# Two weight scalings moved, the first row tile's normalization split, and the last output tiles cut and shared out anew

## The chip, the cores and the metric

One core of a Trainium2 chip. The metric is device time in microseconds (us). TensorE is PE in the profile, its weight load PEld, VectorE is DVE, ScalarE ACT, GpSimd POOL, the SyncE queue SP; a "q" behind an engine is its sequencer, which issues transfers and waits.

## The reference

```python
xn = layernorm(x)                                      # x: [2048, 640] bf16
q  = (xn @ wq) as 32 heads of 192
s  = softmax(q k^T * 192**-0.5) v over the last 512 keys, all heads, then @ wo      # [2048, 640]
g  = silu( (sigmoid(xn @ w_gate) * (xn @ w_up)) @ w_down )
return x + s * g
```

## The kernel before

It starts with the gate branch (first four row tiles normalized and turned one by one, then the weights), goes through the query projection and attention in 16 rounds, and ends with the products with `wo` for the last eight row tiles. `row tile` is 128 rows of 640 columns. What the change touches:

```python
# start: row tile 0..3
def ln_apply(t):
    xn = xpool.tile([P, D], BF16, name="xn")
    nc.vector.tensor_scalar(xn[:], x_tiles[t], mv[:, t, 0:1], rstd[:, t, :],
                            op0=ALU.subtract, op1=ALU.mult)
    return xn
...
for q in range(TQ):
    if q + 1 < TQ: ln_part(q + 1, 0)                 # statistics of the next tile, first half
    nc.vector.reciprocal(rstd[:, q:q+1, :], ...)
    xn_t[q] = ln_apply(q)
    if q + 1 < TQ:
        ln_stats(q + 1, 1)                           # second half
        ln_sqrt(q + 1)                               # ScalarE
    if q == 0:
        turn(0); warm_up(NWARM[1]); continue         # TensorE transposes, ScalarE copies them out
...
# weights of the second pair of rounds: VectorE scales a chunk, GpSimd builds the sums, and loads
def scale_raw(g, c, on_act=True): ...                # 128x1536, bf16 -> fp16, in place
def second_w(c):
    copy_w(1, c, nc.gpsimd.tensor_copy)
    sum_w(1, c, nc.gpsimd.tensor_tensor, nc.gpsimd.tensor_copy)
    load_raw(1 + (c + 3) // NCD, (c + 3) % NCD, nc.gpsimd)
...
for n, k in enumerate((0, 1, 7, 2, 3, 8, 4, 5, 9, 6, 10)):   # query products of the first round
    slots[k]()
    if n == 2: ...
    elif n == 6:
        scale_raw(1, 2, on_act=False)
    if n in (0, 1, 6):
        second_w(min(n, 2))
...
    for k, x in enumerate(s_list):                   # score steps, with the next round's query products
        stage_s(r, *x, k)
        ...
        if r == 0 and k in (3, 7):
            scale_raw(1, 3 + k // 4, on_act=False)
            second_w(3 + k // 4)
...
# end
def finish(ps, gB_sb, t, d0, d1, on_pool=False, queue=nc.sync):
    o_sb = late["fout"].tile([P, D], BF16, name="o_sb")        # four buffers
    d = slice(d0, d1)
    if on_pool:
        tmp = late["tmp"].tile([P, D], F32, name="tmp")
        nc.vector.tensor_tensor(tmp[:, d], ps, gB_sb[:, d], ALU.mult)
        nc.gpsimd.tensor_tensor(o_sb[:, d], tmp[:, d], acc[t][:, d], ALU.add)
    else:
        nc.vector.tensor_tensor(ps, ps, gB_sb[:, d], ALU.mult)
        nc.vector.tensor_tensor(o_sb[:, d], ps, acc[t][:, d], ALU.add)
    queue.dma_start(of[t * P:(t + 1) * P, d], o_sb[:, d])

def stage_wo(r, i, q):
    ...
    if r == last and i * TQ + q == 2 * TQ - 1:       # the eighth of the last tiles, in three pieces
        cuts = [0, D // 2, D - P, D]
        for e, (d0, d1) in enumerate(zip(cuts, cuts[1:])):
            ps = ps_all[:, (4, 5, 0)[e], 0:d1 - d0]
            wo_mm(ps, r, i, q, [(d0, d1 - d0)], d0)
            finish(ps, gates[t], t, d0, d1, queue=nc.scalar)
        return
    ...                                              # GpSimd adds tiles 2, 4, 6 and 7 of the last eight
```

The softmax here doesn't subtract the row's maximum and nothing guards it: scores larger than these inputs give would overflow.

## Time and profile before

| before | |
|---|---|
| time, median of the first 3 runs | 905.09 us (904.78 to 905.09) |
| span of the profiled run | 902.9 us |
| TensorE busy | 896.0 us (99%) |
| first matmul at / last one ends at | 1.34 / 898.40 us |
| last transfer lands / program ends | 901.59 / 902.85 us |

An engine at 99% sets the time, so only its gaps count. If the middle hangs on TensorE alone, a gap that is closed early should arrive at the end in full.

### The profile page before, as it was taken

What the parts mean: (1) busy time and instruction counts of PE and PEld (TensorE: products, weight loads), DVE (VectorE), ACT (ScalarE), POOL (GpSimd) and SP (SyncE); (2) the same over time, 40 slices, a digit from 0 to 9 for tenths busy, and PEclk for the clock granted to TensorE, in tenths of its full rate; (3) what the DMA queues carried; (4) which work ended last, traced back from release to release, by engine and by line L of the source; (5) the groups of instructions that cost most, each with busy time, mean ns of one, the idle gap of its engine ahead of it and who ended that gap; (6) DMA issues with size and microseconds to landing.
All of it is one profiled execution on the core that took longest, in us unless ns stands there. A gap on an engine that the chain in (4) does not pass through costs nothing. (4 is left out here: it accounts for less than half of the span.)

```text
span 902.9 us, 18554 instructions
## 1 busy us (share of the span) xinstructions
PE 896.0 (99%) x7791; PEld 531.6 (59%) x7791; DVE 653.0 (72%) x1090; ACT 432.9 (48%) x511; POOL 178.8 (20%) x220
## 2 busy tenths in 40 slices
PE   9999999999999999999999999999999999999998
PEld 5545454556656565656565656566666666565665
DVE  5879956677677867786778677866786678666566
ACT  4323346764247633753376437643854285424240
POOL 0051112780001100110011001100110000001982
PEclk9999999999999999999999999999999999999999
DMA  9993384424554645373626362727293815263744
GB/s 284 269 268 92 97 146 104 119 55 87 87 91 59 144 76 102 60 143 69 109 56 147 57 119 46 157 54 123 31 172 45 132 23 129 39 120 130 159 128 121
DMA packets 188069, 100.38 MB, mean 111 GB/s; under 512 B 156176, under 2 KB 180368, under 8 KB 187984
## 3 DMA queue, kind: packets, MB, share of 16 engines
q1 hardware_dynamic: 158656, 57.69, 32.5%
q0 software_dynamic: 9408, 29.93, 14.2%
q10 hardware_dynamic: 19920, 11.57, 5.5%
q8 instruction: 61, 1.00, 0.5%
q14 instruction: 24, 0.20, 0.1%
HBM read 57.87 MB, written 5.24 MB: 70 GB/s over the span
## 5 line engine op out<-in xcount | busy, mean ns | idle before, releaser
L657 ACT ACTIVATE E<-ps_all 128x1024 bf16<-128x1024 f32 x256 | 252.7, 1022 | 303.0 <-PE ps_all L653 184.8
L714 PE MATMUL ps_all<-wo_g,oT 128*128 128x512 bf16 (+2 forms) x1542 | 228.3, 299 | 0.0
L653 PE MATMUL ps_all<-qT,kT 64*128 64x512 bf16 x1536 | 194.4, 376 | 0.0
L671 PE MATMUL ps_all<-v_sb,E 128*128 128x193 bf16 x2048 | 189.8, 247 | 0.1
L671 PEld LDWEIGHTS <-E 128*128 128x128 bf16 x2048 | 168.6, 98 | 18.7 <-issue 6.8
L714 PEld LDWEIGHTS <-oT 128*128 128x128 bf16 x1542 | 121.5, 98 | 78.4 <-issue 2.3
L584 DVE COPY qp<-ps_all 128x512 f32<-128x512 f32 x150 | 100.7, 688 | 58.4 <-PE ps_all L563 58.3
L601 DVE TENSOR_TENSOR qT<-ps_all,qp 128x512 bf16<-128x512 f32 x165 | 109.7, 688 | 45.7 <-PE ps_all L563 37.4
L653 PEld LDWEIGHTS <-kT 64*128 64x128 bf16 x1536 | 75.4, 94 | 89.2 <-issue 5.2
L678 DVE TENSOR_TENSOR o_st<-ps_all,rden 128x768 bf16<-128x768 f32 x120 | 114.9, 957 | 5.0 <-DMA oT<-o_st 0.9
L202 POOL DMA_DIRECT2D raw<-in_A_wq_dram x80 | 48.1, 606 | 276.2 <-ACT wB L224 238.9
L135 POOL DMA_DIRECT2D k_sb<-in_A_k_cache_dram x32 | 32.7, 1026 | 275.2 <-DVE o_st L678 155.6
L219 ACT ACTIVATE raw<-raw,w_sc 128x1536 f16<-128x1536 bf16 x37 | 58.3, 1575 | 1.9 <-DMA raw<-in_A_wq_dram 1.0
L497 PE MATMUL ps_all<-wd_sb,hT_sb 128*128 128x512 bf16 (+1 forms) x384 | 52.8, 299 | 0.0
L563 PE MATMUL ps_all<-XA,wA 64*128 64x512 f16 x420 | 51.9, 376 | 0.2 <-DVE qp L584 0.2
L563 PE MATMUL ps_all<-XB,wB 64*128 64x512 f16 x420 | 52.0, 376 | 0.0
L563 PE MATMUL ps_all<-X,w 64*128 64x512 bf16 x420 | 51.9, 376 | 0.0
L749 DVE TENSOR_TENSOR acc_lo<-ps_all,acc_lo 128x640 f32<-128x640 f32 x48 | 39.5, 823 | 15.9 <-PE ps_all L714 15.7
L453 DVE TENSOR_TENSOR hT_sb<-ps_all,sig_sb 128x512 bf16<-128x512 f32 x48 | 32.4, 683 | 22.0 <-ACT sig_sb L452 11.3
L677 DVE RECIPROCAL rden<-ps_all 128x4 f32<-128x4 f32 x128 | 23.2, 181 | 34.1 <-PE ps_all L671 32.7
L452 ACT ACTIVATE sig_sb<-ps_all 128x512 bf16<-128x512 f32 x48 | 28.0, 596 | 40.1 <-PE ps_all L447 37.1
L749 DVE TENSOR_TENSOR acc_hi<-ps_all,acc_hi 128x640 f32<-128x640 f32 x48 | 39.3, 819 | 7.7 <-PE ps_all L714 7.7
(118 smaller groups left out, 764.0 us busy)
## 6 DMA issues: line engine op xcount, KB each, us to landing
raw<-in_A_wq_dram POOLq DMA_DIRECT2D x80, 192.0 KB, 4.1
k_sb<-in_A_k_cache_dram POOLq DMA_DIRECT2D x32, 192.0 KB, 5.6
wo_g<-in_A_wo_dram ACTq DMA_DIRECT2D x6, 960.0 KB, 7.1
v_sb<-in_A_v_cache_dram ACTq DMA_DIRECT2D x28, 192.0 KB, 3.8
gB_d<-gB_sb POOLq DMA_DIRECT2D x16, 160.0 KB, 3.5
gBa_sb<-gB_d SPq DMA_DIRECT2D x16, 160.0 KB, 3.9
xa_sb<-in_A_x_dram SPq DMA_DIRECT2D x16, 160.0 KB, 3.9
out_dram<-o_sb SPq DMA_DIRECT2D x15, 160.0 KB, 1.9
```

The source lines that it names most:

```text
L202: eng.dma_start(raw[r], wq_r[:, c, :, g * GC:(g + 1) * GC])
L219: nc.scalar.activation(raw.bitcast(F16), raw, AF.Copy, scale=w_up)
L497: nc.tensor.matmul(oB_ps[:, d0:d0 + dsz], lhsT=hT_sb[:, f, q * P:(q + 1) * P], rhs=wd_sb[:, f, d0:d0 + dsz], start=(f == 0), stop=(f == NF ...
L563: nc.tensor.matmul(ps_all[:, b, :], lhsT=w(r, c), rhs=x[r, c, :], start=(first and k == 0), stop=(k == len(cs) - 1), skip_group_check=True,)
L584: nc.vector.tensor_copy(dst, part(b))
L601: nc.vector.tensor_tensor(q_out(i, u, pp), part(b), t, ALU.add)
L653: nc.tensor.matmul(ps[:, b, :], lhsT=kT[h, c * PC + j, :], rhs=qT_t[r][i, j][h, pp, :], start=(j == 0), stop=(j == PC - 1),)
L657: nc.scalar.activation(E_t[r, i, pp][:, c, :, :], ps, AF.Exp, scale=scale_qk)
L671: nc.tensor.matmul(o_ps[:, q // 2, q % 2, 0:DH + 1], lhsT=E[:, c, h, q * P:(q + 1) * P], rhs=vt[:, c, 0:DH + 1], start=(c == 0), stop=(c = ...
L678: nc.vector.tensor_tensor(o_st[:, :, h * DH:(h + 1) * DH].rearrange("p (b i) d -> p b i d", b=2), o_ps[:, :, :, 0:DH], rden[:].to_broadcas ...
L714: nc.tensor.matmul(oA[:, d0 - base:d0 - base + dsz], lhsT=oT_t[r, i, pp][:, q * PC + j, :], rhs=wo_t[runs[r][1]][:, cc, d0:d0 + dsz], star ...
L749: nc.vector.tensor_tensor(acc[t][:], oA[:, 0:D], acc[t][:], ALU.add)
```

## The change

The intent: take two scalings out of the way of bank evacuations that TensorE waits for, let the first transposes start before the whole tile is normalized, and shorten the work behind the last matmul.

```diff
         def ln_apply(t):
             xn = xpool.tile([P, D], BF16, name="xn")
-            nc.vector.tensor_scalar(xn[:], x_tiles[t], ...)
+            cuts = [0, 2 * P, D] if t == 0 else [0, D]
+            for d in map(slice, cuts, cuts[1:]):
+                nc.vector.tensor_scalar(xn[:, d], x_tiles[t][:, d], ...)
 ...
+    tail_of = {n: ([0, D], (None,), (n in (1, 3, 4),)) for n in range(5)}
+    tail_of[5] = [0, D // 2, D], (6, 7), (False, False)                  # cuts, banks, addition on GpSimd
+    tail_of[6] = [0, D // 2, D], (2, 3), (True, True)
+    tail_of[7] = [0, D // 2, D - P, D], (4, 5, 0), (True, False, False)
 ...    (stage_wo walks these; one o_sb and one tmp tile per row tile; the pieces of the
 ...     eighth tile go out on ScalarE's queue unless GpSimd adds them)
-        elif n == 6:
-            scale_raw(1, 2, on_act=False)
-        if n in (0, 1, 6):
-            second_w(min(n, 2))
+        if n < 2:
+            second_w(n)
+    scale_s = {0: 2, 3: 3, 15: 4}
 ...
-            if r == 0 and k in (3, 7):
-                scale_raw(1, 3 + k // 4, on_act=False)
-                second_w(3 + k // 4)
+            if r == 0 and k in scale_s:
+                scale_raw(1, scale_s[k], on_act=False)
+                second_w(scale_s[k])
```

More of the change, by code (lines that the diff above doesn't have):

```diff
@@ L336, in ln_apply @@
             xn = xpool.tile([P, D], BF16, name="xn")
-            nc.vector.tensor_scalar(
-                xn[:], x_tiles[t], mv[:, t, 0:1], rstd[:, t, :],
-                op0=ALU.subtract, op1=ALU.mult,
-            )
+            cuts = [0, 2 * P, D] if t == 0 else [0, D]
+            for d in map(slice, cuts, cuts[1:]):
+                nc.vector.tensor_scalar(
+                    xn[:, d], x_tiles[t][:, d], mv[:, t, 0:1], rstd[:, t, :],
+                    op0=ALU.subtract, op1=ALU.mult,
+                )
             return xn
@@ L718, in wo_mm, with finish @@
                 )
-    def finish(ps, gB_sb, t, d0, d1, on_pool=False, queue=nc.sync):
-        o_sb = late["fout"].tile([P, D], BF16, name="o_sb")
-        d = slice(d0, d1)
-        if on_pool:
-            tmp = late["tmp"].tile([P, D], F32, name="tmp")
-            nc.vector.tensor_tensor(tmp[:, d], ps, gB_sb[:, d], ALU.mult)
+    def finish(ps, t, d, o_sb, tmp=None, queue=nc.sync):
+        if tmp is None:
+            nc.vector.tensor_tensor(ps, ps, gates[t][:, d], ALU.mult)
+            nc.vector.tensor_tensor(o_sb[:, d], ps, acc[t][:, d], ALU.add)
+        else:
+            nc.vector.tensor_tensor(tmp[:, d], ps, gates[t][:, d], ALU.mult)
             nc.gpsimd.tensor_tensor(o_sb[:, d], tmp[:, d], acc[t][:, d], ALU.add)
-        else:
-            nc.vector.tensor_tensor(ps, ps, gB_sb[:, d], ALU.mult)
-            nc.vector.tensor_tensor(o_sb[:, d], ps, acc[t][:, d], ALU.add)
         queue.dma_start(of[t * P:(t + 1) * P, d], o_sb[:, d])
+    tail_of = {n: ([0, D], (None,), (n in (1, 3, 4),)) for n in range(5)}
+    tail_of[5] = [0, D // 2, D], (6, 7), (False, False)
+    tail_of[6] = [0, D // 2, D], (2, 3), (True, True)
+    tail_of[7] = [0, D // 2, D - P, D], (4, 5, 0), (True, False, False)
     def stage_wo(r, i, q):
@@ L734, in stage_wo @@
         t = row_tile(r, i, q)
-        if r == last and i * TQ + q == 2 * TQ - 1:
-            cuts = [0, D // 2, D - P, D]
-            for e, (d0, d1) in enumerate(zip(cuts, cuts[1:])):
-                ps = ps_all[:, (4, 5, 0)[e], 0:d1 - d0]
-                wo_mm(ps, r, i, q, [(d0, d1 - d0)], d0)
-                finish(ps, gates[t], t, d0, d1, queue=nc.scalar)
-            return
-        oA = flat(bank2())
-        wo_mm(oA, r, i, q, d_chunks)
-        if g == NG - 1:
-            finish(oA[:, 0:D], gates[t], t, 0, D, r == last and (q % 2 == 1 or (i, q) == (1, 2)))
-        elif g == 0:
-            nc.vector.tensor_copy(acc[t][:], oA[:, 0:D])
-        else:
-            nc.vector.tensor_tensor(acc[t][:], oA[:, 0:D], acc[t][:], ALU.add)
+        if g < NG - 1:
+            oA = flat(bank2())
+            wo_mm(oA, r, i, q, d_chunks)
+            if g == 0:
+                nc.vector.tensor_copy(acc[t][:], oA[:, 0:D])
+            else:
+                nc.vector.tensor_tensor(acc[t][:], oA[:, 0:D], acc[t][:], ALU.add)
+            return
+        cuts, banks, pool_adds = tail_of[i * TQ + q if r == last else 0]
+        o_sb = late["fout"].tile([P, D], BF16, name="o_sb")
+        tmp = late["tmp"].tile([P, D], F32, name="tmp") if any(pool_adds) else None
+        for d0, d1, b, on_pool in zip(cuts, cuts[1:], banks, pool_adds):
+            if b is None:
+                ps = flat(bank2())[:, 0:D]
+                wo_mm(ps, r, i, q, d_chunks)
+            else:
+                ps = ps_all[:, b, 0:d1 - d0]
+                wo_mm(ps, r, i, q, [(d0, d1 - d0)], d0)
+            by_act = len(banks) == 3 and not on_pool
+            finish(ps, t, slice(d0, d1), o_sb, tmp if on_pool else None, nc.scalar if by_act else nc.sync)
     runs = [(pi, g) for g in range(NG) for pi in range(2)]
```

## The prediction

> **What bounds the kernel now.** I read four views of the profile of before: the page's busy times, the list of waits of TensorE, the timeline of the stretches where TensorE waits, and the timeline of the last microseconds. The page and the waits come first.
>
> ```profile
> PE 896.0 (99%) x7791; PEld 531.6 (59%) x7791; DVE 653.0 (72%) x1090; ACT 432.9 (48%) x511; POOL 178.8 (20%) x220
> ...
> engine line waited for: us in total, times, longest us
> PE ps_all L350 <- DVE warm L344: 1.3, 1, 1.3
> PE ps_all L563 <- DVE qT L601: 0.4, 1, 0.4
> PE ps_all L360 <- ACT X L375: 0.3, 1, 0.3
> PE ps_all L563 <- DVE qp L584: 0.2, 1, 0.2
> ```
>
> TensorE is busy for 896.0 of 902.9 us. Nothing is to be had in the middle of the kernel except where TensorE itself waits, and that is three short waits besides the start: two of the query products (L563) for VectorE and one in the first row tiles (L360). The other idle time is before the first matmul (1.34 us) and behind the last one (4.5 us). The change touches exactly these places, and it adds or removes no matmul column: it is worth fractions of a microsecond out of 905.
>
> The two query waits, in the timeline:
>
> ```profile
> 172.01 1.29 DVE L601 TENSOR_TENSOR qT<-ps_all,acc_lo 128x512 bf16<-128x512 f32 x2 [3.07 <-PE ps_all L563]
> 173.22 0.61 DVE L221 TENSOR_SCALAR raw<-raw,w_sc 128x1536 f16<-128x1536 bf16 x1
> 173.74 3.08 DVE L601 TENSOR_TENSOR qT<-ps_all,acc_lo 128x512 bf16<-128x512 f32 x5
> 175.68 0.80 PE L563 MATMUL ps_all<-XC,wC 64*128 64x512 bf16 x5 [0.45 <-DVE qT L601]
> ...
> 190.66 1.26 DVE L221 TENSOR_SCALAR raw<-raw,w_sc 128x1536 f16<-128x1536 bf16 x1
> 191.84 0.68 DVE L584 COPY qp<-ps_all 128x512 f32<-128x512 f32 x1
> 192.57 1.25 PE L563 MATMUL ps_all<-XA,wA 64*128 64x512 f16 x10 [0.18 <-DVE qp L584]
> ```
>
> In both a weight scaling (L221) on VectorE stands in front of the bank evacuations, and TensorE waits for an evacuation behind it. The bracket understates the loss, because a matmul counts as busy for 0.25 us after its slot. Ten such matmuls take 1.08 us of issue: those from 173.90 leave the engine free at 174.98, and the next starts at 175.68, which is 0.70 lost. Twelve take 1.30: those from 190.92 end at 192.22, and the next start at 192.57, 0.35 lost.
>
> The end:
>
> ```profile
> 896.13 3.17 POOL L726 TENSOR_TENSOR o_sb<-tmp,acc_hi 128x640 bf16<-128x640 f32 x2 [1.77 <-DVE tmp L725]
> 896.86 0.82 DVE L725 TENSOR_TENSOR tmp<-ps_all,gBa_sb 128x640 f32<-128x640 f32 x1 [0.81 <-PE ps_all L714]
> 897.61 0.50 DVE L728 TENSOR_TENSOR ps_all<-ps_all,gBa_sb 128x320 f32<-128x320 f32 x1
> ...
> 898.14 0.49 DVE L729 TENSOR_TENSOR o_sb<-ps_all,acc_hi 128x320 bf16<-128x320 f32 x1
> 898.55 0.35 DVE L728 TENSOR_TENSOR ps_all<-ps_all,gBa_sb 128x192 f32<-128x192 f32 x1
> 898.66 1.66 ACTq L730 DMA_DIRECT2D out_dram<-o_sb  x3
> 898.94 0.36 DVE L729 TENSOR_TENSOR o_sb<-ps_all,acc_hi 128x192 bf16<-128x192 f32 x1
> 899.21 0.29 DVE L728 TENSOR_TENSOR ps_all<-ps_all,gBa_sb 128x128 f32<-128x128 f32 x1
> 899.66 0.29 DVE L729 TENSOR_TENSOR o_sb<-ps_all,acc_hi 128x128 bf16<-128x128 f32 x1 [0.16 <-DVE ps_all L728]
> ```
>
> The last matmul ends at 898.40, but VectorE has work back to back until 899.95; its last piece is written out by a DMA issued at 899.98 and landed at 901.59. The program ends 1.26 us behind that landing (902.85). Two more landings are close: 901.41 (the 192 columns) and 901.23 (GpSimd's seventh tile). The last addition also waits 0.13 us for an output buffer: the chain of waits leads from it to the landing at 899.48 of the sixth tile, since the three pieces of the eighth take three of four buffers.
>
> **What the Trainium skill says.** "VectorE: DVE Perf Modes", section "The TRN2 errata", gives (N+151)/0.96 ns for an fp32 tensor_tensor; that is 824, 491, 357 and 291 ns for 640, 320, 192 and 128 columns, and the trace has 825, 491, 358 and 291. "TensorE: Matmul & The Clock Gate", section "Back-to-back issue gap", gives N/2.4 + 2.5 ns warm: six pairs of 512 and 128 columns are 1.63 us, twelve of 320 are 1.63 us too; the trace has 1.63 for the first, and 0.136 from one 320-column matmul to the next. So cutting a tile into halves costs TensorE nothing. "GPSIMD Engine Reference", section "Specifications", says that GpSimd shares its SBUF interfaces with VectorE's two-port modes; the trace agrees in the scaling, 0.61 us while GpSimd only issues transfers, 0.89 and 1.26 while it adds. "DMA: Bandwidth & Descriptors", section "Anatomy of one DMA", puts the fixed cost near 2.0 us, mostly the receipt (it says so of GpSimd's own path); the last transfers here, from the other queues, took 1.61 us (32 KB), 2.08 (48 and 80 KB), 1.78 to 1.90 (160 KB).
>
> **The scalings, part by part.** First: chunk 2's scaling leaves the place ahead of the five additions for the start of the first score stage. It held VectorE for 0.52 us (173.22 to 173.74). The third of the five, for which TensorE waits, now ends 0.52 earlier, at 175.10 and not 175.62; TensorE starts at 175.15 instead of 175.68. It still waits 0.17, because the additions themselves run behind. The next dependence, the first product of the following query at 177.75 behind the addition at 177.01, moves by the same 0.52. At its new place, about 177.2, VectorE has 1.32 us of idle time ahead of its next copy (179.03 before), so 0.9 us fit, and GpSimd takes the chunk up only at 181.1. Gain 0.52.
>
> Second: chunk 4's scaling goes from the eighth to the last score step. The copy behind it can run when its product is ready, about 0.27 behind the slot's end (189.84 + 1.08 + 0.27 = 191.19), not at 191.84, and the whole 0.35 goes. At its new place, about 199.4, GpSimd is idle (so 0.61 us) and VectorE idles 1.02 us there. GpSimd's work on chunk 4, from 195.80 to 201.4, now begins near 200.0 and ends near 205.7; its first product is at 210.9. Gain 0.35. From here TensorE is continuous to the end, so I carry 0.87 through in full.
>
> **The first row tile.** Its normalization (0.45 us) becomes 256 and 384 columns. The warm-up matmuls keep TensorE until 4.73 + 0.43 = 5.16, and the first transpose is at 5.23, so at most 0.07 is to be had there. But ScalarE copies the transposes only behind its square root for the second tile (5.85), which VectorE feeds, and a second instruction delays that by some 0.03 to 0.06. The reciprocal at 6.30 stands behind a statistics step that waits for its input's DMA at 5.89, which takes the delay up again; TensorE's next wait, 8.55, is on that chain. Net 0.00, at most 0.07 either way.
>
> **The last tiles.** GpSimd had whole tiles 2, 4, 6, 7 (counting from one). Now it has 2, 4, 5, both halves of 7, and the first 320 columns of 8; VectorE has both halves of 6. A product is ready for VectorE about 0.1 us behind the modelled end of its last matmul. Independent 320-column operations follow each other by 0.41, dependent ones by 0.53. This gives: tile 6 at 894.42, 894.95, 895.36, 895.90; tile 7 at 896.31 and 896.86, ending 897.36; tile 8's first product at 897.61 as before, since TensorE sets it. Then the 192 columns at 898.12 and 898.51 (to 898.87), and the 128 at 898.79 and 899.11 to 899.40 instead of 899.95: one addition of 0.49 is gone, and the buffer wait with it (one output tile per row tile). The last 32 KB then land at 899.43 + 1.61 = 901.04, the 48 KB at 898.90 + 2.08 = 900.98.
>
> GpSimd becomes the later one. Its 640 columns take 1.54, so a half is 0.77, with 0.09 between two: 896.89 to 897.65, 897.74 to 898.51, and tile 8's piece 898.60 to 899.37. The SP queue issues that at 899.40, and 80 KB land in 1.78 to 2.08 (I take 1.85, nearer to SP's own): 901.25. Against 901.59 that is 0.34.
>
> Sum: 0.52 + 0.35 + 0.00 + 0.34 = 1.21 us; 905.09 - 1.21 = 903.9.
>
> **Rivals.** (1) GpSimd's chain is longer than I think: a fixed cost in each half, or slowed beside VectorE. For it: three halves in a row leave it no idle time. Against: 384 columns in 16-bit took 0.91 and 640 in fp32 1.54, a line through nearly zero. With 0.15 more in each, the last landing is that of before, and the time 904.2. (2) The recovered time is lost again further on, since VectorE is 72% busy and TensorE meets the next late evacuation 0.5 us sooner. Against: the trace has no other wait of TensorE there; evacuations that follow TensorE shift with it. It would leave 904.7. (3) Chunk 4's weights come too late for the next query's product. Against: 5 us to spare; if a transfer in GpSimd's queue held it, it would cost some microseconds: 907. (4) The split tile is worth more, because an earlier start shifts the clock's warm-up. At most 0.2.
>
> **Range and chances.** The three runs of before spread over 0.31 us. The tail may be 0 to 0.5, the scalings 0.5 to 0.95, the start ±0.07. Together 903.2 to 904.9. Two per cent are 18 us; neither the removable waits nor anything that the change adds comes near: 0.99 for the same.
>
> **What would show it.** In the changed profile: the wait for the addition near 175 shrinks to under 0.2 in slots (perhaps not listed), the one near 192 is gone, and the stretch from the first score step to the next output product starts 0.87 earlier; scalings of some 0.6 to 0.9 near 177 and 199.5 with no wait of TensorE around 210; the first products unchanged within 0.07 at 8.5; VectorE ending 1.0 us after the last matmul and not 1.55; three GpSimd additions of 0.77 back to back, and the last landing from the SP queue. It would be wrong if TensorE lists a new wait on VectorE or GpSimd, if the last DMA lands over 3.2 us after the last matmul as now, or if the whole difference is under 0.4 us.

## The result, and the profile after

The changed kernel took 903.38 us (903.27 to 903.84, 6 runs), the kernel before in its 6 runs 904.88 (904.63 to 905.09): 1.50 us less, ratio 0.9984 with a 95% interval of 0.9971 to 0.9997; within 2% that counts as the same. Ratios here are the mean time of one kernel's fast runs over that of the other's of the same rounds, so not quite the ratio of the medians. The granted clock of the profiled ones was 0.999 to 1.0.

The page's first line and the list of TensorE's waits, of the changed kernel (columns as before):

```profile
PE 895.3 (99%) x7791; PEld 531.9 (59%) x7791; DVE 652.5 (72%) x1093; ACT 432.9 (48%) x511; POOL 179.9 (20%) x222
...
PE ps_all L352 <- DVE warm L346: 1.3, 1, 1.3
PE ps_all L362 <- ACT X L377: 0.5, 2, 0.3
```

Both waits of the query products for VectorE are gone. The wait of the first row tiles (L362) is still there, twice now. The timeline of the stretch, changed kernel (start, duration, engine, line, operation; in brackets the idle time before it and what ended it):

```profile
172.06 4.28 DVE L603 TENSOR_TENSOR qT<-ps_all,acc_lo 128x512 bf16<-128x512 f32 x7 [3.06 <-PE ps_all L565]
...
173.95 2.05 PE L565 MATMUL ps_all<-XC,wC 64*128 64x512 bf16 x15
...
177.14 0.84 DVE L221 TENSOR_SCALAR raw<-raw,w_sc 128x1536 f16<-128x1536 bf16 x1
...
191.73 1.26 PE L565 MATMUL ps_all<-XA,wA 64*128 64x512 f16 x10
...
198.53 0.61 DVE L221 TENSOR_SCALAR raw<-raw,w_sc 128x1536 f16<-128x1536 bf16 x1
...
199.21 1.06 POOL L228 COPY acc_hi<-raw 64x384 f16<-64x384 f16 x2 [3.44 <-DVE raw L221]
```

The seven additions (L603) run without the scaling in their middle, the fifteen products follow without a bracket, and the products at 191.73 have lost theirs. The scalings stand at 177.14 (foreseen 177.2) and 198.53 (foreseen 199.4), and take 0.84 and 0.61. The last tiles:

```profile
895.18 1.06 DVE L728 TENSOR_TENSOR tmp<-ps_all,gBa_sb 128x320 f32<-128x320 f32 x2
895.74 2.50 POOL L729 TENSOR_TENSOR o_sb<-tmp,acc_hi 128x320 bf16<-128x320 f32 x3 [0.73 <-DVE tmp L728]
896.64 0.49 DVE L728 TENSOR_TENSOR tmp<-ps_all,gBa_sb 128x320 f32<-128x320 f32 x1 [0.39 <-POOL o_sb L729]
897.06 0.37 DVE L725 TENSOR_TENSOR ps_all<-ps_all,gBa_sb 128x192 f32<-128x192 f32 x1
897.46 0.36 DVE L726 TENSOR_TENSOR o_sb<-ps_all,acc_hi 128x192 bf16<-128x192 f32 x1
897.74 0.29 DVE L725 TENSOR_TENSOR ps_all<-ps_all,gBa_sb 128x128 f32<-128x128 f32 x1
897.85 0.90 ACTq L730 DMA_DIRECT2D out_dram<-o_sb  x2
898.06 0.29 DVE L726 TENSOR_TENSOR o_sb<-ps_all,acc_hi 128x128 bf16<-128x128 f32 x1
```

The last matmul ends at 897.36 here and at 898.40 before; VectorE ends 0.99 us behind it, not 1.55. The three GpSimd additions take 2.50 together. One bracket must be read with care: the product at 896.64 is put down to GpSimd, but the last matmul of that piece ended at 896.53, and 0.1 behind it is where such a product starts elsewhere too. TensorE held it.

**Where the 1.39 us between the two traces (902.85 to 901.47) came from.** I compared the same ScalarE activations in both traces, and from 898 us on the last matmul, landing and end. "Start" is the shift at 164 to 172 us, "scalings" what comes to it until 205, "middle" from there to the last matmul, "end" the change of the time from the last matmul to the program's end, which is 4.46 in the kernel before (negative is sooner):

| | start | scalings | middle | end | sum |
|---|---|---|---|---|---|
| changed kernel | +0.05 | -0.88 | -0.20 | -0.35 | -1.39 |
| predicted | 0.00 | -0.87 | 0 | -0.34 | -1.21 |

The middle was not in the prediction: near 704 us a scaling of keys on VectorE waits for its transfer, landed at 703.58, and TensorE's next products stand behind VectorE. In the changed kernel the transfer landed 0.14 sooner, measured against TensorE's own shift there. The runs below show this term in kernels without the change too.

### The profile page after: what moved, and what is told of

It reads as the page before. It is cut to its first block, busy times and chain, and to the rows that moved or that the text cites. A ratio compares the mean times of both kernels' runs of the same rounds, so it can differ in the third digit from the quotient of the medians.

```text
span 901.5 us, 18561 instructions
## 1 busy us (share of the span) xinstructions
PE 895.3 (99%) x7791; PEld 531.9 (59%) x7791; DVE 652.5 (72%) x1093; ACT 432.9 (48%) x511; POOL 179.9 (20%) x222
## 4 chain that ended last, share of the span: by engine, by line
PE 98%; DVE 1%; DMA 0%; ACT 0%; SPq 0%; issue 0%; POOL 0%; DVEq 0%
PE ps_all L716 23%; PE ps_all L565 20%; PE ps_all L673 19%; PE ps_all L655 18%; PE ps_all L449 11%; PE ps_all L499 6%; PE ps_all L362 1%; DMA x_sb<-in_A_x_dram 0%; ACT E L659 0%; DVE tmp L728 0%; DVE ps_all L725 0%; DVE o_sb L726 0%; SPq L297 0%; DVE stats L324 0%; POOL o_sb L729 0%
## 5 line engine op out<-in xcount | busy, mean ns | idle before, releaser
L603 DVE TENSOR_TENSOR qT<-ps_all,qp 128x512 bf16<-128x512 f32 x165 | 109.7, 688 | 46.0 <-PE ps_all L565 39.4
```

What stands on the lines that cost most here:

```text
L603: nc.vector.tensor_tensor(q_out(i, u, pp), part(b), t, ALU.add)
```

## The experiments

All twelve gave correct results. The timed intervals are about ±0.0013 of the time, that is ±1.2 us, wider than most of the differences; so the verdicts rest on the traces, and the medians are only asked whether they agree. The same split of each profiled run, against the profiled run of before:

| run | median (before in its rounds) | ratio, 95% | start | scalings | middle | end | sum |
|---|---|---|---|---|---|---|---|
| a1_scalings | 904.10 (904.77) | 0.9993, 0.9981 to 1.0006 | +0.11 | -0.88 | +0.02 | +0.06 | -0.69 |
| a2_split | 905.66 (904.77) | 1.0009, 0.9996 to 1.0021 | +0.41 | -0.02 | -0.13 | +0.78 | +1.04 |
| a3_tail | 904.55 (904.77) | 0.9996, 0.9983 to 1.0010 | +0.20 | +0.02 | -0.21 | -0.34 | -0.32 |
| a4_no_split | 903.95 (904.77) | 0.9991, 0.9978 to 1.0003 | +0.58 | -0.88 | -0.21 | -0.30 | -0.81 |
| c0_after_again | 903.57 (904.80) | 0.9987, 0.9975 to 1.0000 | +0.07 | -0.89 | -0.27 | -0.18 | -1.26 |
| c1_split_buf6 | 904.97 (904.80) | 1.0004, 0.9990 to 1.0017 | +0.15 | +0.03 | -0.17 | -0.01 | 0.00 |
| b3_first_piece_dve | 903.40 (904.80) | 0.9984, 0.9972 to 0.9997 | +0.11 | -0.88 | -0.15 | -0.56 | -1.48 |
| c3_x_early | 903.34 (904.80) | 0.9985, 0.9972 to 0.9997 | -0.13 | -0.88 | -0.21 | -0.35 | -1.57 |
| c4_x_early_split | 903.56 (904.97) | 0.9984, 0.9972 to 0.9997 | +0.23 | -0.89 | -0.03 | -0.30 | -0.98 |
| b1_chunk2 | 904.15 (904.97) | 0.9991, 0.9977 to 1.0005 | +0.45 | -0.83 | -0.21 | +0.25 | -0.34 |
| d2_x_early_dve | 903.59 (904.97) | 0.9983, 0.9971 to 0.9996 | +0.29 | -0.89 | -0.02 | -0.39 | -1.00 |
| d3_two_queues | 903.69 (904.97) | 0.9985, 0.9972 to 0.9999 | +0.32 | -0.88 | -0.17 | +0.11 | -0.63 |

**The parts alone.** `a1_scalings` is the kernel before with only the last two hunks of the diff, `a2_split` with only the first, `a3_tail` with only the tail hunks, `a4_no_split` the changed kernel with

```diff
-            cuts = [0, 2 * P, D] if t == 0 else [0, D]
+            cuts = [0, D]
```

> The kernel before with the moved scalings alone. My theory (each part stands by itself, TensorE carries it to the end): 0.9 us less than before, that is 0.54 at the query product near 175.7 and 0.36 near 192.6, and nothing else moves before 700 us. Rival (VectorE loses part of it again further on, or a later k-cache landing takes it): under 0.6 us less, with a new listed wait of TensorE on VectorE. Second rival (the late weights of chunk 4): a wait of TensorE near 210.

> The kernel before with the split first row tile alone. My theory from the trace of the changed kernel (the two pieces hold VectorE 0.55 us where the one held it 0.36, and everything of the second tile stands behind it): the third product of the first tile and the product near 8.5 us start 0.16 us later, of which the input's transfer may hide up to 0.1; the whole kernel 0.05 to 0.17 us slower. Rival (the prediction: taken up by the wait for the transfer): within 0.03 in the trace. Rival of the change's intent: 0.05 or more faster.

> The kernel before with the new last tiles alone. My theory: VectorE ends 1.0 us behind the last matmul and not 1.55; the last landing is only about 0.05 to 0.35 us nearer to the last matmul, because GpSimd's three halves take 0.86 each and the last transfers about 2.0 to 2.2 us; the program's end 0.35 us nearer to the last matmul, part of it because fewer semaphores are still to be looked at behind the last landing. The time 0.2 to 0.5 us less than before. Rival (GpSimd is the bound and gives it all back): within 0.1 us of before.

> The changed kernel without the split of the first row tile. My theory: 0.05 to 0.17 us faster than the changed kernel, so 1.55 to 1.7 us less than before: better than both. Rival (the split is neutral or helps): the same as the changed kernel, 1.5 us less than before, or worse.

The scalings are worth 0.88 us in the trace (0.88 to 0.89 in all nine profiles that move both), with no new wait near 210, and nothing of it is lost behind them; of the 0.9 expected, 0.88 is near enough, and the rivals fall. The tail gives 0.34 alone and 0.30 to 0.35 with the rest, but only 0.18 in the second profile of the changed kernel (`c0` below). The split alone was 0.9 slower in the timed runs, far above what was expected, and most of it (0.78) sat at the *end*, in code that the split does not touch. And `a4_no_split` was not better than the changed kernel: its start was 0.58 late, because its third row tile landed at 6.56 us where the changed kernel's landed at 6.03. In `a2_split` the product near 8.5 was 0.19 later, near the expected 0.16, but then the fourth tile set the start: it landed at 8.49 instead of 8.08, its statistics waited for it, and the start is 0.41 late; in `b1_chunk2`, without a split, the same at 8.53 (+0.45). So the start column measures when the first row tiles land, more than it measures the split. That called for the next four.

**The changed kernel once more, unedited:**

> The changed kernel once more, unedited, for comparison with the others on one chip. If the landing times of the first row tiles belong to the program: the third row tile lands near 6.03 us and the start costs 0.05 us against before, 1.4 us less in the trace, 1.5 in the timed runs. If they belong to the single execution or the chip: the third tile lands anywhere between 5.7 and 6.6, the start costs up to 0.5 and the gain is 0.9 to 1.5.

Start +0.07, third tile landed at 6.05, 1.23 us less in the timed runs. The landing is near the first profile's 6.03, while the other eight profiled kernels with this order of loads had it from 5.73 to 6.56. It came back in the same program; whether it belongs to the program or to chance, two profiles don't settle.

**Six output buffers beside the split:**

```diff
-            for name, n in (..., ("fout", 4), ...):
+            for name, n in (..., ("fout", 6), ...):
```

> The kernel before with the split first row tile and six output buffers instead of four. The split alone was 0.9 us slower, and its trace puts 0.8 of this at the end: the last addition waits for an output buffer whose transfer landed 2.86 us after its issue and not 1.78, behind an 8 KB instruction fetch. My theory (the buffer wait is the cause): VectorE ends 1.42 us behind the last matmul whatever the landings, instead of 2.63, and 0.7 to 1.0 us less than the split alone. Rival (the late landing itself, or the split, makes the end late): VectorE still ends over 2 us behind the last matmul.

The last VectorE lines of the split alone:

```profile
899.47 0.29 DVE L730 TENSOR_TENSOR ps_all<-ps_all,gBa_sb 128x128 f32<-128x128 f32 x1
901.00 0.29 DVE L731 TENSOR_TENSOR o_sb<-ps_all,acc_hi 128x128 bf16<-128x128 f32 x1 [1.24 <-issue]
```

and with six buffers:

```profile
899.22 0.29 DVE L730 TENSOR_TENSOR ps_all<-ps_all,gBa_sb 128x128 f32<-128x128 f32 x1
899.54 0.29 DVE L731 TENSOR_TENSOR o_sb<-ps_all,acc_hi 128x128 bf16<-128x128 f32 x1
```

The wait is gone: the sixth tile's transfer landed only 1.49 us behind the last matmul, and the addition had already run at 1.14, which four buffers would not have allowed. VectorE ends 1.43 us behind the last matmul and not 2.63, and the end column goes from +0.78 to -0.01, the timed median from 0.89 above before to 0.17 above. The theory holds. "Issue" in the bracket is a buffer wait that the profile could not put down to anything: the third piece of the eighth tile takes the buffer of the sixth, whose transfer landed 2.86 us after its issue instead of 1.78. The packets in the trace of the split alone (no view of the profile prints them) show part of why that one was late: of its 16 closing packets (4 bytes each) fifteen came between 0.57 and 0.73 us behind the last matmul, the sixteenth at 1.12, at the very end of an 8 KB packet of the instruction queue (0.81 to 1.12). In `a1_scalings` the same fetch began at 0.86, when all sixteen were through (0.73), and the transfer landed in 1.78. The sixteenth packet accounts for 0.39 of the 1.07 us. The rest lies behind it: the semaphore counted the other fifteen 0.33 to 0.35 us after their packets, this one 1.03 after. That the fetch held it up, on one of the DMA engines, is inferred from these times; the packets of the trace carry no engine. The run with six buffers doesn't test it, since its fetch came elsewhere (-0.05 to 0.26). If it is so, a fetch that began 0.04 us sooner cost the old tail over 1 us, through one buffer.

So the four buffers were a hazard of the kernel before, worth 0.12 us of VectorE's end in its profile (1.55 against 1.43) and 1.2 in another build. The change removes it as a side effect, since a row tile now takes one buffer and not three.

**The eighth tile's first piece back on VectorE:**

```diff
-    tail_of[7] = ..., (4, 5, 0), (True, False, False)
+    tail_of[7] = ..., (4, 5, 0), (False, False, False)
```

> The changed kernel with the first 320 columns of the eighth tile added on VectorE again. My theory (VectorE is the bound of the last microsecond): VectorE ends 1.42 us behind the last matmul and not 0.99 (one addition of 0.49 more, less a short wait), the last landing 0.1 to 0.4 us later, the time 0.1 to 0.4 us above the changed kernel. Rival 1 of the prediction (GpSimd's chain is the bound): the same or faster than the changed kernel, since GpSimd then ends about 0.8 us earlier.

My forecast fell, and the rival's came true. VectorE did end at 1.43 as expected, but the program ended 3.89 us behind the last matmul, sooner than the 4.11 and 4.28 of the two profiles of the changed kernel. The rival's reason doesn't hold all the same: in the changed kernel GpSimd's piece landed at 2.93, ahead of ScalarE's last at 3.12. The last transfers of this run, as issued:

```profile
897.74 1.53 ACTq L730 DMA_DIRECT2D out_dram<-o_sb  x3
...
898.61 0.29 DVE L726 TENSOR_TENSOR o_sb<-ps_all,acc_hi 128x128 bf16<-128x128 f32 x1
```

Its three pieces were issued 0.27, 0.93 and 1.46 us behind the last matmul and took 2.09, 1.77 and 1.46 to land; those of the changed kernel 0.49, 0.91 and 1.02, and took 2.25, 2.03 and 2.10. The last piece was issued 0.44 later and landed 0.20 earlier (2.92 against 3.12). Compare also `c1_split_buf6`: it issues its three pieces at the same 0.27, 0.93 and 1.46, and differs in that tile 7's 160 KB are issued at 0.93 among them, where this run issued their two halves at -0.73 and 0.09; its last landing is 3.34.

The counts on the semaphores say more. A transfer has landed when its semaphore has been counted up sixteen times, and the trace has the time of each count. For the last transfer of each kernel, in us behind the last matmul:

| profile | issued | 14 of 16 counts by | the sixteenth | last 8 KB instruction fetch before it |
|---|---|---|---|---|
| before | 1.58 | 3.15 | 3.20 | 0.86 to 1.39 |
| changed kernel | 1.02 | 2.75 | 3.12 | 1.54 to 1.99 |
| changed kernel again, `c0` | 1.03 | 2.77 | 3.31 | 1.47 to 2.11 |
| `b3` | 1.46 | 2.88 | 2.92 | 1.52 to 1.89 |
| `c1` | 1.46 | 3.32 | 3.34 | 2.68 to 2.98 |
| `d2`, below | 1.46 | 2.88 | 3.10 | 1.47 to 2.14 |
| `d3`, below | 1.46 | 2.98 | 3.58 | 1.48 to 2.62 |

So two things set this end. The bulk of the last transfer is through 0.40 sooner in the changed kernel than before, and 0.13 later than that in `b3` and `d2`: for the bulk my theory held, VectorE's end counts. It also counts that tile 7 is out early (0.44 between `c1` and `b3`). But one or two counts of the sixteen come up to 0.6 late, and they hide it: `b3` landed sooner because it had nearly no straggler. In the six profiles with the changed last tiles (the two in the table, `a3`, `a4`, `c3` and `c4`) the last landing, 3.12 to 3.31, goes up with the end of a second instruction fetch, 1.99 to 2.11. In the kernel before this fetch came after all landings (3.95). That the fetch makes the stragglers is inferred from this, as in `c1` above; no run moves the fetch alone. One profile stands behind each row.

**The row tiles loaded earlier:**

```diff
-        load_x(0); load_x(1)
+        for t in range(3): load_x(t)
         for k in ...:  load_w(wg_sb, wg_r, k); load_w(wu_sb, wu_r, k)
-            if k < 2: load_x(2 + k)
+            if k < 1: load_x(3 + k)
```

without the split (`c3_x_early`) and with it (`c4_x_early_split`):

> The changed kernel without the split, and with the third and fourth row tiles loaded one place earlier in the queue of loads (ahead of the first and second weight pieces). My theory (the landing of the third row tile sets the start, not the split): it lands near 5.0 to 5.5 us, VectorE does not wait for it, the product near 8.5 us comes 0.2 to 0.4 us earlier than in the changed kernel, unless the first weight pieces (used from 6.5 us on, landing at 4.8 and 5.6 now, then near 5.5 and 6.2) become the wait. Rival (VectorE's own work sets the start): within 0.1 us of the changed kernel at 8.5 us.

> The changed kernel, split kept, with the third and fourth row tiles loaded one place earlier. In the same order of loads without the split the third tile landed at 4.93 us, and nothing hides VectorE's work any more. My theory (the split holds VectorE 0.19 us longer): against that kernel the copies of the second tile start 0.15 to 0.2 later (7.93 to 7.98 and not 7.78), and everything behind by 0.1 to 0.2; the time 0.1 to 0.2 us above its 903.34. Rival (the split is free, or gains the 0.07 of the earlier first transpose): equal to it within 0.05 in the trace at 8 to 12 us.

The third tile now landed at 4.93 and 4.91, and VectorE's own work shows. In `c3` the product near 8.5 came 0.18 sooner than in the changed kernel (8.53 against 8.71), between theory and rival, since the weights became the wait. Without the split, with it:

```profile
4.73 0.45 DVE L339 TENSOR_SCALAR xn<-x_sb,mv,rstd 128x640 bf16<-128x640 bf16 x1
...
5.09 0.48 DVE L324 BATCH_NORM_STATS2 stats<-x_sb 128x6 f32<-128x320 bf16 x1
...
7.78 0.70 ACT L377 ACTIVATE X<-ps_all 128x640 bf16<-128x640 bf16 x1
```

```profile
4.73 0.63 DVE L339 TENSOR_SCALAR xn<-x_sb,mv,rstd 128x256 bf16<-128x256 bf16 x2
...
5.29 0.48 DVE L324 BATCH_NORM_STATS2 stats<-x_sb 128x6 f32<-128x320 bf16 x1
...
7.96 0.70 ACT L377 ACTIVATE X<-ps_all 128x640 bf16<-128x640 bf16 x1
```

The second tile's copies are 0.19 later with the split, just what VectorE is held longer by: from the first piece to the next operation it is 0.55 instead of 0.36. So the split costs 0.19 where it isn't hidden. In the changed kernel it is hidden, because VectorE then waits for the third tile anyway. Here too TensorE did not feel it: with the early loads it waits for the weights (its product at 8.23 in the first, at 8.60 in the second stands behind a landing of the up-projection weights, at 8.19 and 8.56). These landings, not the split, make the 0.36 between the two in the start column. The timed medians are 903.34 and 903.56, from different chips; `d2_x_early_dve`, which has no split and ran beside the second, took 903.59. The split neither helps nor hurts measurably.

**Chunk 2's scaling alone:**

```diff
+        if n < 2: second_w(n)
+    scale_s = {0: 2, 3: 3, 7: 4}          # chunk 4 stays at the eighth step
```

> The kernel before with only the scaling of chunk 2 moved. My theory (the two waits are separate): the query product near 175.7 comes 0.52 earlier, the wait near 192.6 stays at 0.35; 0.5 us less than before at 205 us. Rival (the later wait comes of the earlier one): 0.87 less.

The rival won. The first wait went as predicted (0.52), but the second nearly went with it:

```profile
190.58 0.96 DVE L221 TENSOR_SCALAR raw<-raw,w_sc 128x1536 f16<-128x1536 bf16 x1
...
191.46 0.68 DVE L584 COPY qp<-ps_all 128x512 f32<-128x512 f32 x1
192.19 1.26 PE L563 MATMUL ps_all<-XA,wA 64*128 64x512 f16 x10
```

Chunk 4's scaling is at its old place, but takes 0.96 us and not 1.26, because GpSimd's additions stand elsewhere. GpSimd in the kernel before, and here:

```profile
190.59 0.91 POOL L238 TENSOR_TENSOR acc_hi<-acc_hi,raw 128x384 f16<-128x384 f16 x1
```

```profile
190.22 0.91 POOL L237 TENSOR_TENSOR acc_hi<-raw 128x384 f16<-128x384 f16 x1
```

In the 14 traces 23 of the 42 scalings of this kind took 0.61 us. The other 19 started while GpSimd was adding or copying and had more than 0.19 us of that instruction still ahead; all 19 ended 0.41 to 0.42 behind the end of that instruction, and took 0.80 to 1.29. So a scaling waits out the GpSimd instruction that it meets. In the kernel before it began (190.66) just behind the start of an addition, which ended at 191.50; here (190.58) it met the one before, which ended at 191.12. GpSimd works through the chunks in order, and with chunk 2 handed to it later its additions stand later against TensorE. The copy ends in time, and of the 0.35 only 0.06 is left (the twelve matmuls before end their slots at 190.83 + 1.30 = 192.13). So in this order 0.83 of the 0.88 come of moving chunk 2; moving chunk 4 buys the rest, and independence from what GpSimd does at that moment. Chunk 4 moved alone was not run; if it gives the 0.35 by itself, the two shares overlap.

**The combinations:**

> What the runs point to as best: no split, earlier loads of the row tiles, moved scalings, new last tiles but the eighth wholly on VectorE. If the gains add: the start of the kernel with earlier loads (1.2 us less at the last matmul than before) and the end of the one with VectorE (3.89 us behind the last matmul): 1.8 us less than before, 903.0. Rival (the end at 3.89 was an accident of the landings): 903.3 to 903.5, with the last landing over 3.1 us behind the last matmul.

> The same, with the second piece of the eighth tile (192 columns) issued from the SP queue, the first and third from ScalarE's. If a queue's order held the landings: the last landing 0.1 to 0.3 us sooner. If only the nearness in time of the transfers counts[...]: the same within 0.1.

`d2` joins no split, early loads and the eighth tile on VectorE; `d3` also issues the second piece from SP (`by_act = len(banks) == 3 and b != 5`). Neither is better than its parts: 903.59 and 903.69. `d2` fell short of the 903.0 and did as its rival said. In `d2` the fourth row tile and the next weights landed 0.4 to 0.6 us later than in `c3`, so the start gave nothing; its end, 4.07, is between b3's 3.89 and the changed kernel's. In `d3` the transfer issued on SP took 2.47 and the last one landed at 3.58, 0.48 later than in `d2`, but 14 of its 16 counts only 0.10 later (table above): the lateness is the stragglers', beside a fetch of 1.14 us. The second queue does not help, and one profile does not tell whether it harms. I have no version that is clearly faster than the changed kernel: the best medians, 903.34 and 903.40, differ from its own two, 903.38 and 903.57, by less than the runs of one kernel spread.

## Why the prediction was right, and where its steps were not

The time was 903.38 for a predicted 903.9, inside 903.2 to 904.9, and the same within 2%. Some luck is in the number: in the trace the change's own terms (scalings and end) are 1.23 for a predicted 1.21, and 0.20 more came from a middle that is not the change's. By its steps:

- **TensorE carries the gain to the end**: right. The scalings' 0.87 were 0.88 in the trace, and nothing ate them (rival 2 and rival 3 fell; GpSimd took up chunk 4 at 199.21 and the next query product did not wait).
- **Its split into 0.52 and 0.35**: the sum right, the second term wrongly put down. I took the two scalings for separate causes; the run with chunk 2 alone shows that the second wait went mostly with the first, through the scaling's duration beside GpSimd. The prediction quoted 0.61, 0.89 and 1.26 us for that very operation and did not ask what would make it 1.26 there again.
- **The first row tile**: net 0.00 was right, and so was the reason, the landing of the third tile. The size was wrong: VectorE is held 0.19 longer, not 0.03 to 0.06. I had taken the duration to shrink with the columns; 256 columns took 0.345 us, 384 0.373 and 640 0.446, so most of it is fixed. Rival 4 (the split is worth more, by an earlier start) fell: the first transpose is 0.07 earlier (5.15), as the prediction allowed, and nothing of it arrives.
- **The last tiles**: the sum was 0.34 and measured 0.35, but that is luck: two of its terms missed and cancelled, and the second profile of the changed kernel gave 0.18. VectorE's end (1.0 predicted, 0.99) and GpSimd's (0.97 predicted, 0.88) were right; a half on GpSimd takes 0.86, not 0.77, made up by an earlier start. The last landing was not 0.34 but 0.08 nearer to the last matmul (3.12 against 3.20). It was ScalarE's 32 KB and not SP's piece, and took 2.10 and not 1.61: most of its counts took 1.73, the third of three transfers issued within 0.53 us, and the last straggled by 0.37. In place of that, the program ended 0.98 behind the last landing and not 1.26: SP's sequencer looks at the semaphores one after another, some 0.06 each, and five such looks stood behind the last landing before, two after. All eight other profiles with the new last tiles, `b3` and `d2` among them, ended 0.97 to 0.99 behind theirs, so this part is the steady one. The formula that the prediction cites for TensorE is, on its page, that of a single matmul; for a stream the page has less, 131 ns at 512 columns. The stream here followed the formula (1.63 us for six pairs).
- **Rival 1** ("the last landing is that of before") came true in the landing, 0.08 against 0.34, but not by GpSimd's chain; the stragglers did it. The prediction's own sign of being wrong, a last landing over 3.2, came up in `c0` (3.31).
- **Not foreseen**: 0.2 us in the middle. Ten of the thirteen other profiled runs have 0.13 to 0.27 of it, among them three with neither scaling moved (a2, a3, c1); three have none (a1, c4, d2), two of which contain most of the change. It goes with the landing of the keys: against TensorE's own shift they landed within 0.03 us of before's time in the three that have none, 0.07 to 0.11 sooner in a2, b3 and c1 (0.13 to 0.17), and 0.14 to 0.43 sooner in the rest (0.17 to 0.27). So it does not go with a part of the change. Why the keys land differently is open.

## What to carry to other kernels

Look for what holds an engine's *neighbours*: an operation that waits nowhere can still stretch beside another engine (0.61 to 1.29 us here), and moving one such operation can free a second wait further on, so test the parts singly before crediting each. Behind the last matmul, get the large transfers out first, and take a landing apart before you explain it: here one late count of sixteen hid what the bulk of the transfer had gained. And count buffers by pieces, not by tiles: a fourth buffer that is nearly always free cost 1.2 us of VectorE's end when one landing was late.

## What the Trainium skill lacked or had wrong

- "Runtime: NRT & Kernel Launch", section "Instruction fetch mechanics", says that the sequencers fetch their instructions in 16 KiB blocks over their own DMA queue and calls the fetch hidden. For the engine that fetches this may be so; the section does not say what it does to other transfers. Here an 8 KB fetch goes with a landing of 2.86 us instead of 1.78, and in the kernel before a 16 KB fetch of 1.57 us with one of 3.92 us: fifteen closing packets by -4.92 us against the last matmul, the sixteenth at -2.91. That the one makes the other is inferred, not shown.
- "DMA: Bandwidth & Descriptors", section "Anatomy of one DMA", gives a fixed cost near 2.0 us, for GpSimd's path. The same 32 KB took 1.46 to 2.28 us here, issued by ScalarE, with what else was under way; the section gives no spread for that.
- "GPSIMD Engine Reference", section "3.1 Elementwise — side-by-side cycle accounting", has 2.6 cycles for an element of two inputs; 320 and 640 columns (fp32 in, bf16 out) took 0.86 and 1.54 us, which is, by an estimate from these two with the page's 1.2 GHz, 2.55 cycles and a fixed part of 0.18 us per instruction. The section gives no figure for the latter.
- The same page, section "Specifications", names the contention with VectorE but gives it no size there: one scaling of 128x1536 took 0.61 us alone and 0.80 to 1.29 beside GpSimd, ending 0.41 to 0.42 behind the GpSimd instruction that it met, and a GpSimd addition 0.91 alone and up to 1.23.
- "VectorE: DVE Perf Modes", section "The TRN2 errata": the fp32 formula held to the nanosecond, but for the bf16 tensor_scalar with two pointer scalars the fixed part is larger than its 58 cycles, and than the 150 it measured: 0.345 us for 256 columns and 0.446 for 640 leave, by an estimate, 0.28 us, some 267 cycles at the page's 0.96 GHz.
